# Port-order waits between VectorE and GpSimd, kept for the first half of the execution only, in a two-layer attention and MLP kernel

## The chip, the cores and the metric

The kernel runs on one core of a Trainium2 chip. A core has five engines with a queue of instructions each: TensorE (matrix products; the profile calls it PE, and its weight loads PEld), VectorE (DVE), ScalarE (ACT), GpSimd (POOL) and SyncE (SP), which here issues the DMAs. An engine works its own queue strictly in order; engines meet only through semaphores. SBUF is the on-chip memory that all of them use, PSUM the banks into which TensorE writes its products. The metric is the device time of one execution in microseconds (us), the median of several runs.

## The reference

Two kinds of layer alternate, attention (A) and MLP (B), each run twice with the same weights; the input `x` is 2048 tokens of 512 features in bf16.

```
def A(x, wqkv, wo):          # 32 heads of 16 features
    q, k, v = split(x @ wqkv)
    scores = (q . k) / 4
    mask: 0 <= query - key < 256         # a sliding window
    return softmax(masked scores) @ v, heads joined, @ wo
def B(x, w1, b1, w2, b2):    # 1792 hidden features
    return gelu(x @ w1 + b1) @ w2 + b2

x = x + A(layernorm(x)); x = x + B(layernorm(x))
x = x + A(layernorm(x)); x = x + B(layernorm(x))
```

## The kernel before, in words

The tokens are handled in 16 blocks of 256 (two tiles of 128), eight for each of the two layers. For a block, attention goes through *visits*. A visit computes 512 columns of scores for four heads at a time (TensorE, line 765), exponentiates them from PSUM into the SBUF tile `E` (ScalarE, two instructions of line 772), and multiplies the pieces of `E` at the window's edge with a 0/1 mask (line 793). That mask product reads two SBUF tiles, `E` and `mask01`. It runs on VectorE or, for the instructions listed in `_ALT`, on GpSimd. Then the probabilities meet the values (TensorE, line 817), VectorE transposes the result into `OD` (826), takes reciprocals of the sums (830), and `Nb = OD * Rc` is formed (834; VectorE or GpSimd). A transpose gives `OT` (840), and TensorE multiplies it with `Wo_sb` (line 664, as all the projections and the MLP). VectorE adds that to the residual `X` (866).

Layer norm is `bn_stats` and `bn_aggr` (616, 618, VectorE), the addition of epsilon (622; VectorE or GpSimd), a power of -0.5 on GpSimd (628), and the normalized tile `xn` on VectorE (638). `xn` is transposed by DMA (643), for the first and last tiles by TensorE (650) with a copy out of PSUM (605). The MLP's hidden tile `gT` gets bias and gelu on ScalarE (897), or bias on VectorE (889) and gelu on ScalarE (892). Its output is added on VectorE (909) to `Xb`, which GpSimd has prepared as `X` plus the bias `b2` (905).

The order of the work is written out. `_ORDER` is the order in which the 3080 steps are recorded, and with it each engine's queue; `_ALT` names the steps that go to the other engine; `_BANKS` the PSUM banks. The recording layer then puts a semaphore wait ahead of each instruction that reads or overwrites what another engine has made, unless an earlier wait already covers it.

`_TURNS` adds waits to this that no data needs. It is a flat list of pairs (a, z) of step numbers. For each pair, a is made to write a name that z reads, so that z waits for the end of a. In each pair one step is on VectorE and the other on GpSimd, and z is the later one in `_ORDER`. Nearly all the pairs are among mask products (793), `xn` (638), `Nb` (834), the epsilon step (622) and `Xb` (905). A step in several pairs stands in the list several times.

```
for a, z in zip(_TURNS[0::2], _TURNS[1::2]):
    nodes[a]["writes"] = nodes[a]["writes"] + ["turn%d" % z]
    nodes[z]["reads"] = nodes[z]["reads"] + ["turn%d" % z]
    nodes[z]["deps"].add(a)
```

Of the kernel before, what the change touches and what calls it, by code (L numbers as in the profile page):

```python
# [19 lines left out]
class _Sched:  # L20
# [339 lines left out]
]  # L360

_BANKS = [
# [618 lines left out]
```

## Time and profile before

| | |
|---|---|
| median of 3 runs | 440.76 us (440.29 to 441.36) |
| profiled execution | 440.62 us, of which the instructions span 438.9 us |
| busy: TensorE / ScalarE / VectorE / GpSimd | 424.2 / 385.6 / 341.0 / 201.1 us |
| TensorE clock granted | full throughout |
| mask products (793): VectorE / GpSimd | 122 with 51.0 us / 114 with 120.3 us |
| `xn` (638, VectorE), `Xb` (905, GpSimd) | 64 with 24.5 us / 32 with 36.8 us |

A row of the timeline gives the start (us from the span's start), the length, the engine, the line, the operation, the tiles written and read (out<-in) with their shapes, and how many instructions of that kind follow each other; in brackets, the engine's idle time before it and who ended it. A row of the groups by shape gives the count, total busy us and mean ns of one, and the idle time before these instructions with what ended it. A row of the waits gives who waited for whom, us in total, how many times, and the longest. "TENSOR_TENSOR E<-E,mask" is the mask product; its shape tells how many columns of `E` it covers.

### The profile page before, as it was taken

Reading aid. Unit: us, or ns where it says so; the run is one execution under the profiler, and the core shown is the slowest. Engines: PE = TensorE matmul, PEld = TensorE weight load, DVE = VectorE, ACT = ScalarE, POOL = GpSimd, SP = SyncE. Lnnn points to the kernel's source line nnn. Section 1 sums busy time; section 2 is a strip of 40 time slices with the busy share of each in tenths; the row PEclk is TensorE's granted clock in tenths of the full one; section 3 lists DMA queues with packets and bytes.
Section 4 is the critical chain, followed back from the end, with each engine's and each line's share of the span. In section 5 each row is a group of like instructions: output and inputs, shape, how many; then the busy total and the mean of one; then the engine's idle time right before and its main releaser. Section 6 shows DMA issues by size and latency. Waiting matters only on the chain.

```text
span 438.9 us, 16940 instructions
## 1 busy us (share of the span) xinstructions
PE 424.2 (97%) x7579; PEld 230.4 (52%) x7579; DVE 341.0 (78%) x647; ACT 385.6 (88%) x457; POOL 201.1 (46%) x224
## 2 busy tenths in 40 slices
PE   8989999999699989999999999999999999999997
PEld 4555756554344554454455555454564554544763
DVE  5999987799686889876899797877877686754852
ACT  3899999999999899999999988899888979899632
POOL 4366136464550275451854437743454515625222
PEclk9999999999999999999999999999999999999999
DMA  7772912002200102311030211201232022101011
GB/s 236 210 203 50 227 39 56 15 21 64 48 1 14 32 16 48 50 33 25 10 74 9 37 29 27 52 1 33 58 45 69 1 33 63 47 0 28 15 48 49
DMA packets 47972, 23.25 MB, mean 53 GB/s; under 512 B 33180, under 2 KB 47900, under 8 KB 47900
## 3 DMA queue, kind: packets, MB, share of 16 engines
q1 hardware_dynamic: 47900, 22.17, 21.8%
q8 instruction: 60, 0.98, 0.9%
q14 instruction: 12, 0.10, 0.1%
HBM read 8.00 MB, written 2.10 MB: 23 GB/s over the span
## 4 chain that ended last, share of the span: by engine, by line
PE 84%; ACT 8%; DVE 4%; DMA 3%; issue 1%; SPq 1%; POOL 0%; DVEq 0%
PE ps L664 65%; PE ps L765 10%; PE ps L817 8%; ACT E L772 7%; DMA W_sb<-in_B_w_dram 1%; DMA xnTB<-xn 1%; DVE stat L616 1%; DVE OD L826 1%; DVE KT L698 1%; DMA X<-in_A_x_dram 0%; PE ps L650 0%; DVE xn L638 0%; DVE X L909 0%; DVE X L866 0%; SPq L643 0%
## 5 line engine op out<-in xcount | busy, mean ns | idle before, releaser
L772 ACT ACTIVATE E<-ps 128x1024 bf16<-128x1024 f32 x300 | 283.2, 1040 | 25.6 <-PE ps L765 24.8
L793 POOL TENSOR_TENSOR E<-E,mask 128x512 bf16<-128x512 bf16 (+2 forms) x114 | 120.3, 1069 | 132.5 <-ACT E L772 52.7
L664 PE MATMUL ps<-W_sb,gT 128*128 128x512 bf16 x448 | 114.8, 380 | 0.1
L664 PE MATMUL ps<-xnTB,W_sb 128*128 128x512 bf16 (+1 forms) x560 | 109.3, 337 | 1.9 <-ACT E L772 1.5
L664 PEld LDWEIGHTS ps<-xnTB,W_sb 128*128 128x128 bf16 x560 | 51.9, 98 | 43.4 <-issue 4.6
L664 PE MATMUL ps<-xnTA,Wqkv_sb 128*128 128x256 bf16 x512 | 71.6, 273 | 1.2 <-ACT E L772 0.9
L765 PE MATMUL ps<-QT,KT 32*128 32x128 bf16 (+3 forms) x1920 | 60.4, 231 | 4.6 <-ACT E L772 2.6
L664 PEld LDWEIGHTS ps<-W_sb,gT 128*128 128x128 bf16 x448 | 39.4, 98 | 42.8 <-issue 4.0
L793 DVE TENSOR_TENSOR E<-E,mask 128x512 bf16<-128x512 bf16 (+2 forms) x122 | 51.0, 445 | 13.8 <-ACT E L772 11.6
L664 PEld LDWEIGHTS ps<-xnTA,Wqkv_sb 128*128 128x128 bf16 x512 | 46.6, 98 | 22.6 <-issue 3.3
L765 PEld LDWEIGHTS ps<-QT,KT 32*128 32x128 bf16 x1920 | 28.4, 92 | 52.6 <-ACT E L772 34.5
L826 DVE STREAM_TRANSPOSE OD<-ps 128x1024 f32<-128x1024 f32 x32 | 40.0, 1249 | 16.5 <-PE ps L817 14.6
L897 ACT ACTIVATE gT<-ps,b1T 128x512 bf16<-128x512 f32 (+1 forms) x80 | 43.0, 606 | 9.1 <-PE ps L664 9.0
L889 DVE TENSOR_SCALAR gT<-ps,b1T 128x512 bf16<-128x512 f32 (+1 forms) x60 | 36.7, 631 | 11.9 <-PE ps L664 11.4
L616 DVE BATCH_NORM_STATS2 stat<-X 128x6 f32<-128x512 bf16 x64 | 43.6, 687 | 3.0 <-DMA X<-in_A_x_dram 2.2
L905 POOL TENSOR_TENSOR Xb<-X,b2all 128x512 f32<-128x512 bf16 x32 | 36.8, 1154 | 13.1 <-DVE X L909 6.4
L817 PE MATMUL ps<-E,Va 64*17 64x256 bf16 (+3 forms) x1920 | 41.0, 230 | 1.8 <-DVE Va L605 0.5
L698 DVE TENSOR_TENSOR KT<-ps,parmask 128x1024 bf16<-128x1024 f32 x32 | 38.7, 1213 | 5.2 <-PE ps L664 5.0
L817 PE MATMUL ps<-E,Vs 64*17 64x192 bf16 (+3 forms) x1920 | 42.2, 230 | 0.0
L628 POOL TENSOR_TENSOR rstd<-rstd,mhalf 128x2 f32<-128x2 f32 (+1 forms) x33 | 24.2, 734 | 27.6 <-DVE rstd L622 23.3
L817 PEld LDWEIGHTS ps<-E,Va 64*17 64x17 bf16 x1920 | 29.2, 84 | 11.9 <-issue 8.3
L664 PE MATMUL ps<-Wo_sb,OT 128*128 128x512 bf16 x128 | 35.3, 380 | 0.1
(51 smaller groups left out, 350.1 us busy)
## 6 DMA issues: line engine op xcount, KB each, us to landing
Vs<-Va SPq DMA_DIRECT2D x64, 68.0 KB, 2.7
W_sb<-in_B_w_dram SPq DMA_DIRECT2D x4, 512.0 KB, 4.6
out_dram<-X SPq DMA_DIRECT2D x16, 128.0 KB, 1.8
X<-in_A_x_dram SPq DMA_DIRECT2D x3, 512.0 KB, 7.9
Wqkv_sb<-in_A_wqkv_dram SPq DMA_DIRECT2D x4, 256.0 KB, 5.5
W_sb<-in_B_w_dram SPq DMA_DIRECT2D x1, 768.0 KB, 5.2
W_sb<-in_B_w_dram SPq DMA_DIRECT2D x2, 384.0 KB, 5.0
Wqkv_sb<-in_A_wqkv_dram SPq DMA_DIRECT2D x1, 512.0 KB, 7.7
```

Of the source, the lines that this page charges most:

```text
L616: add("dve", lambda e, B, t=t, k6=k6: e.bn_stats(stat6[:, k6, :], X[:, t, :]), reads=["X%d" % t], writes=["st%d" % k6], key="bs%d" % (k + j))
L628: add("pool", lambda e, B, j=j, n=n: e.tensor_tensor(out=rstd[:, k + j : k + j + n], in0=rstd[:, k + j : k + j + n], in1=mhalf[:, 0:n], op ...
L664: r = e.matmul(ps[:, B[g][0], cols], lhsT, rhs, start=st, stop=sp)
L698: add("dve", lambda e, B, g=g, i=i: e.tensor_tensor(out=KT[:, kb, 2 * i : 2 * i + 2].rearrange("p c m a q -> p a (c m) q"), in0=ps[:, B[g] ...
L765: x = e.matmul(ps[:, bk[r], o : o + n], KT[rows, kb, c, m].rearrange("p a q -> p (a q)"), QT[rows, c, q : q + n], start=True, stop=True)
L772: add("act", lambda e, B, g_=g_, gi=gi: e.activation(E[:, 2 * gi : 2 * gi + 2, e0 : e0 + 512], ps[:, B[g_][0] : B[g_][0] + 2, :], AF.Exp, ...
L793: fn = lambda e, B: e.tensor_tensor(out=Ew, in0=Ew, in1=Mw, op=ALU.mult)
L817: x = e.matmul(ps[32 * r : 32 * r + VW, B[g][par], c % 2 * 2 * P + lo : c % 2 * 2 * P + hi], V[rows, (2 * b + m // 2) % VR, c * HC + 2 * r ...
L826: add("dve", lambda e, B: e.transpose(OD[:, s].rearrange("p a c q -> p (a c q)"), ps[:, B[g][0] : B[g][0] + 2, :]), reads=["ps:" + g], wri ...
L889: add("dve", lambda e, B, g=g, fc=fc: e.tensor_scalar(out=gT[:, fc, c0 : c0 + M], in0=ps[:, B[g][0], 0:M], scalar1=b1T[:, fc : fc + 1], sc ...
L897: add("act", lambda e, B, g=g, fc=fc: e.activation(gT[:, fc, c0 : c0 + M], ps[:, B[g][0], 0:M], AF.Gelu_apprx_tanh, bias=b1T[:, fc : fc + ...
L905: add("pool", lambda e, B, t=t, xs=xs: e.tensor_tensor(out=Xb[:, xs, :], in0=X[:, t, :], in1=b2all[:], op=ALU.add), reads=["X%d" % t, "b2a ...
```

## The change

The list `_TURNS` is cut after its 86th pair. The 86 pairs that stay lie in the first half of the execution: in the profiled execution of before, the last instruction that waits by one of them starts at 199.5 us, and the first that waited by one of the other 83 starts at 208.8 us. The loop above, `_ORDER`, `_ALT` and `_BANKS` are the same, so every engine has the same instructions in the same order.

```
-    1753, 1481, 1701, 1705, 1491, 1491, 1719, 1257, 1715, 1715, 1796, 1511, 1811, 1800, 1509, 1800, 1801, 1800, 1805,
-    1800, 1806, 1806, 1602, 1820, 1834, 1743, 1839, 1839, 2010, 2012, 2057, 2057, 1843, 1618, 2134, 1618, 2053, 1618,
...
-    2812, 2817, 2812, 2818, 2818, 2807, 2794, 2926, 2926, 2930, 2926, 2717, 2934, 2935, 2934, 2751, 2940, 2944, 2940,
-    2945, 2940, 2838, 2840, 2939, 2840, 2958, 2963, 2949, 2968, 2967, 2997, 2906, 2997, 2889,
+    1753,
 ]
```

By kind, the 83 pairs that go are: mask products on both engines 29, `xn` and a mask product 18, `Xb` and a VectorE step 18, `Nb` and a mask product 10, the epsilon step and a mask product 6, `xn` and `Nb` 2. Some of them put no wait into the program before, because another wait covered them: the waits that VectorE's queue holds on GpSimd go from 89 to 71, those that GpSimd's holds on VectorE from 98 to 71.

5 rows, old and new, of the table _TURNS are left out of this document.

## The prediction

> **What bounds the kernel now.** I read the page first (busy shares, then the chain that ended last), then the busy time of the half that the change touches, its waits, and last the timeline around single instructions.
>
> ```profile
> PE 424.2 (97%) x7579; PEld 230.4 (52%) x7579; DVE 341.0 (78%) x647; ACT 385.6 (88%) x457; POOL 201.1 (46%) x224
> ...
> PE 84%; ACT 8%; DVE 4%; DMA 3%; issue 1%; SPq 1%; POOL 0%; DVEq 0%
> ```
> ```profile
> 208.50:438.90 230.40, 227.06 (x3915) 120.11 (x3913) 167.14 (x312) 195.07 (x232) 106.67 (x105) 1.00 0.16 35
> ```
>
> The second row is the chain's share by engine; the third is the stretch from 208.5 us on: its length, then PE, PEld, DVE, ACT and POOL busy. TensorE sets the end: in that stretch it idles 230.40 - 227.06 = 3.3 us. Its queue has a fixed order, so a result that comes late for one matmul stops all that follow. VectorE (167 of 230 us) and GpSimd (107) have room on average; what counts is whether one of their results comes late for TensorE.
>
> **What the change removes.** Of the 169 pairs 83 go: in the profiled execution the first instruction freed starts at 208.8 us, the last at 424.0 (the list of pairs matched with the trace). Every engine keeps its order and no data wait goes, so unless the engines disturb each other, everything starts as early as before or earlier. What waits cost from 208.5 us on (who waited for whom: us in total, times, longest):
>
> ```profile
> POOL E L793 <- DVE E L793: 34.9, 11, 9.7
> ...
> POOL E L793 <- DVE xn L638: 7.0, 7, 2.5
> ...
> PEld ps L817 <- DVE E L793: 0.8, 2, 0.4
> ...
> PEld ps L817 <- POOL E L793: 0.2, 1, 0.2
> ```
>
> GpSimd's waits are long, but POOL is 0% of the chain: masks that start earlier are worth something only where TensorE waited for a mask. That is 0.8 + 0.2 = 1.0 us in this half, the most that can come back. Since nearly all the masks end before TensorE asks for them, I take 0.
>
> **What takes the waits' place.** They kept GpSimd's tile operations apart from those of VectorE that read two SBUF tiles (mask product, normalization `Nb`) and from the layer-norm `xn`. What happens when such instructions meet is seen at GpSimd's small rsqrt steps (L622, L628), which mostly have no such wait. First their spread (min/median/max ns), then two meetings:
>
> ```profile
> L628 POOL TENSOR_TENSOR rstd<-rstd,mhalf x33: 563/707/1138, 4.1 to 420.2; 128x2 f32<-128x2 f32 x31, 128x1 f32<-128x1 f32 x2
> ```
> ```profile
> L622 POOL TENSOR_SCALAR rstd<-statmv x16: 211/227/562, 3.8 to 354.2; 128x2 f32<-128x2 f32 x15, 128x1 f32<-128x1 f32 x1
> ```
> ```profile
> 319.47 0.42 DVE L793 TENSOR_TENSOR E<-E,mask 128x512 bf16<-128x512 bf16 x1
> ...
> 319.64 0.81 POOL L628 TENSOR_TENSOR rstd<-rstd,mhalf 128x2 f32<-128x2 f32 x1 [3.27 <-DVE rstd L622]
> ...
> 247.25 0.38 DVE L638 TENSOR_SCALAR xn<-X,statmv,rstd 128x512 bf16<-128x512 bf16 x1
> ...
> 247.42 0.29 POOL L622 TENSOR_SCALAR rstd<-statmv 128x2 f32<-128x2 f32 x1 [1.51 <-DVE statmv L618]
> ```
>
> The step that starts 0.17 us into a mask ends 0.56 us after that mask; the one 0.17 us into an `xn` ends 0.08 us after it. The steps are stretched to the end of VectorE's instruction and a rest, up to 1.138 us instead of 0.707. So one holds the other off entirely, at least when VectorE was first. The opposite case, a large GpSimd operation under way when VectorE's comes, does not occur in this trace: the waits prevented it. Its bounds: 0 (GpSimd holds nothing), or all that is left of GpSimd's operation, which is much longer:
>
> ```profile
> L793 POOL TENSOR_TENSOR E<-E,mask 128x512 bf16<-128x512 bf16 x60 | 68.9, 1154 | 62.0 <-ACT E L772 22.0 <-DVE Nb L834 16.3 <-DVE E L793 16.1
> L905 POOL TENSOR_TENSOR Xb<-X,b2all 128x512 f32<-128x512 bf16 x32 | 36.8, 1154 | 13.1 <-DVE X L909 6.4 <-DVE E L793 3.4 <-DVE xnTB L605 2.0
> ...
> L793 POOL TENSOR_TENSOR E<-E,mask 128x768 bf16<-128x768 bf16 x17 | 27.8, 1640 | 32.7 <-DVE E L793 13.7 <-DVE xn L638 9.1 <-ACT E L772 8.7
> ```
>
> I take nearly all of it, because the nearest rows are the same two engines with the roles exchanged and show a full hold. VectorE then stands for up to 1.64 us, with everything queued behind it, also operations that never met GpSimd. A held GpSimd instruction costs 0: it stands for the rest of a VectorE instruction (at most 0.7 us), where it now waits for several; what covers it is GpSimd's own idle time (230 - 107 us), and were that gone, each would cost those 0.7 us. Three groups of matmuls name a wait on GpSimd themselves that they had through VectorE before: the value was reached already, so 0.
>
> The Trainium skill's page "SBUF — State Buffer", section "Who interferes with whom", says the same of both directions: a VectorE instruction with two SBUF inputs contends with a GpSimd one that reads SBUF, and whoever issues first has the shared pair for the whole instruction. By that rule the sum is the forecast below; by the direction that the trace shows alone it would be that of the second rival. The trace agrees with it for VectorE first (0.81 us instead of 0.707), and has no row for GpSimd first.
>
> **Where it reaches TensorE.** Holds that TensorE does not notice are free. I went through the second half for places with little slack behind a VectorE instruction that a freed GpSimd operation can now stand before, and found five.
>
> A, 224 us:
> ```profile
> 223.35 1.14 POOL L628 TENSOR_TENSOR rstd<-rstd,mhalf 128x2 f32<-128x2 f32 x1 [1.85 <-DVE rstd L622]
> 225.08 2.75 POOL L793 TENSOR_TENSOR E<-E,mask 128x768 bf16<-128x768 bf16 x2 [0.59 <-DVE xn L638]
> ...
> 223.85 0.68 DVE L834 TENSOR_TENSOR Nb<-OD,Rc 128x512 bf16<-128x512 f32 x1
> 224.53 0.41 DVE L638 TENSOR_SCALAR xn<-X,statmv,rstd 128x512 bf16<-128x512 bf16 x1
> ...
> 225.45 0.71 DVE L840 STREAM_TRANSPOSE OT<-Nb 128x512 bf16<-128x512 bf16 x1
> ...
> 226.28 1.25 PE L664 MATMUL ps<-Wo_sb,OT 128*128 128x512 bf16 x5
> ```
> Freed, the 768-wide mask asks at 224.49, when the rsqrt ends, before `xn` at 224.53. `xn` waits up to 1.64 us; the transpose behind it ended at 226.16, 0.12 before its matmul. Cost 1.64 - 0.12 = 1.5 us (0 if `xn` wins).
>
> B, 268 us:
> ```profile
> 267.60 0.90 DVE L793 TENSOR_TENSOR E<-E,mask 128x768 bf16<-128x768 bf16 x2 [0.40 <-ACT E L772]
> 268.41 0.68 DVE L605 CAST QT<-ps 128x512 bf16<-128x512 f32 x1
> ...
> 268.64 2.75 POOL L793 TENSOR_TENSOR E<-E,mask 128x768 bf16<-128x768 bf16 x2 [2.90 <-DVE E L793]
> ...
> 269.43 1.04 PE L664 MATMUL ps<-xnTA,Wqkv_sb 128*128 128x256 bf16 x8
> ```
> GpSimd's mask comes in between VectorE's two: the second, and the QT cast behind it, wait some 1.5 us; the cast ended 269.09, 0.34 before the projection that needs its bank. Cost 1.2 us.
>
> C, 337 us:
> ```profile
> 336.44 0.69 DVE L834 TENSOR_TENSOR Nb<-OD,Rc 128x512 bf16<-128x512 f32 x1 [0.96 <-POOL E L793]
> 337.05 0.42 DVE L793 TENSOR_TENSOR E<-E,mask 128x512 bf16<-128x512 bf16 x1
> 337.38 0.70 DVE L840 STREAM_TRANSPOSE OT<-Nb 128x512 bf16<-128x512 bf16 x1
> ...
> 337.54 2.26 POOL L793 TENSOR_TENSOR E<-E,mask 128x768 bf16<-128x768 bf16 x2 [1.14 <-DVE E L793]
> ...
> 337.99 0.81 PE L664 MATMUL ps<-Wo_sb,OT 128*128 128x512 bf16 x3
> ```
> The 768-wide mask no longer waits for VectorE's mask, follows `Nb` at 337.13 and holds that mask, with the transpose behind it, for up to 1.64 us. The transpose ended at 338.08; if the last of the three output-projection matmuls is the first to need it (starts (0.81 - 0.38) / 2 = 0.21 us apart, with 0.38 for one as at D, so 338.42), the slack is 0.34. Cost 1.3 us.
>
> D, 408 us:
> ```profile
> 407.26 1.39 DVE L793 TENSOR_TENSOR E<-E,mask 128x768 bf16<-128x768 bf16 x4
> ...
> 408.79 1.15 POOL L793 TENSOR_TENSOR E<-E,mask 128x512 bf16<-128x512 bf16 x1 [4.70 <-DVE E L793]
> ...
> 411.45 0.63 ACT L892 ACTIVATE gT<-gT 128x512 bf16<-128x512 bf16 x1 [1.25 <-DVE gT L889]
> ...
> 412.41 0.38 PE L664 MATMUL ps<-W_sb,gT 128*128 128x512 bf16 x1
> ```
> GpSimd's mask falls among VectorE's four; the last moves by about 1.15, so do the bias adds, and the gelu that waits for them. It ended at 412.08, 0.33 before the matmul: 0.8 us.
>
> E, 421 us, on the chain itself:
> ```profile
> 420.89 0.74 DVE L638 TENSOR_SCALAR xn<-X,statmv,rstd 128x512 bf16<-128x512 bf16 x2 [0.80 <-POOL rstd L628]
> ...
> 422.87 2.27 POOL L905 TENSOR_TENSOR Xb<-X,b2all 128x512 f32<-128x512 bf16 x2 [2.02 <-DVE xnTB L605]
> ```
> The Xb add now follows the rsqrt that releases `xn` directly, and stands before the first or the second `xn`; TensorE transposes both next. Cost 1.13 us (2.3 if both adds get in).
>
> Sum: 1.5 + 1.2 + 1.3 + 0.8 + 1.1 = 5.9 us. The profiled execution took 440.62 us (span 438.9 and 1.7 around it), 0.14 below the median 440.76: 440.62 + 5.9 = 446.5 us. DMAs, ScalarE's work and bytes are unchanged and cost 0: what is late is the same work, hidden as before.
>
> **The rivals.**
> - A weaker hold: GpSimd holds VectorE for part only, or VectorE wins half the races. 0.2 to 0.6 of 5.9: 1.2 to 3.5 us, 441.8 to 444.1. Against it: L628's maximum is a complete hold.
> - No hold by GpSimd: VectorE goes on beside it. Then the gain's bound remains, 0 to 1.0 us and the noise: 440.0 to 441.4. For it: only VectorE's hold is seen.
> - Faster: GpSimd's masks at A to D end up to 1 us earlier, and this ends TensorE's waits for masks, 1.0 us: 439.6. It decides only if the holds cost TensorE under 0.1 us. Against it: E, where there is nothing to gain and 1.1 to lose.
> - The change does nothing, because the pairs are implied by other waits: partly so, since in the programs VectorE's waits on GpSimd fall only from 89 to 71 and GpSimd's on VectorE from 98 to 71, which leaves 45 waits that do go; where none of these mattered, the time would be the second rival's.
>
> **How the numbers follow.** About 0.2% (0.9 us) is what a measurement can tell from no change. Forecast (near-full hold, 444.1 to 449.3; the upper end takes 1.5, 1.5, 1.6, 1.15 and 2.3 = 8.1, and 0.6 for smaller places): 0.56. Weaker hold 0.18, no hold or no effect 0.16, faster 0.08, above 449.3 0.02. Slower is 0.56 + 0.18 + 0.02 = 0.76. The range leaves out the fastest and slowest ends: 440.3 to 449.3.
>
> **What would show it.** Right: from 208.5 us on, VectorE instructions of the three kinds end with, or just after, a GpSimd operation, or take longer than now; the matmuls at A to E start later by the sums given, in steps; TensorE's idle time in the stretch grows from 3.3 to about 9 us; the first 208 us stay. Wrong: GpSimd's masks overlap VectorE's with unchanged durations, or `xn` at A and E goes first each time.

## The result, and the profile after

| | before | after |
|---|---|---|
| median | 441.01 us (440.29 to 442.90, 6 runs) | 447.56 us (446.89 to 449.50, 6 runs) |
| ratio | | 1.0152, 95% interval 1.0122 to 1.0183 |
| profiled execution (span) | 440.62 (438.9) us | 446.97 (445.2) us |

The change costs 6.5 us by the medians and 446.97 - 440.62 = 6.35 us between the profiled executions; forecast was 5.9. The page of the changed kernel, its lines 8 lower (630 is `xn`, 785 the mask product, 897 `Xb`):

```profile
PE 425.4 (96%) x7579; PEld 230.0 (52%) x7579; DVE 356.0 (80%) x647; ACT 385.9 (87%) x457; POOL 204.0 (46%) x224
...
PE 76%; DVE 11%; ACT 10%; DMA 1%; issue 1%; POOL 1%; SPq 0%; DVEq 0%
...
L785 DVE TENSOR_TENSOR E<-E,mask 128x512 bf16<-128x512 bf16 (+2 forms) x122 | 57.9, 501 | 12.3 <-ACT E L764 12.0
...
L630 DVE TENSOR_SCALAR xn<-X,statmv,rstd 128x512 bf16<-128x512 bf16 x64 | 32.5, 527 | 4.3 <-POOL rstd L620 3.8
```

VectorE is busy for 15.0 us more with the same 647 instructions: 6.9 of them in the mask products (57.9 against 51.0 before) and 8.0 in `xn` (32.5 against 24.5). VectorE's share of the chain went from 4 to 11%. The two halves (length, then PE, PEld, DVE, ACT, POOL busy):

```profile
0.00:208.10 208.10, 196.86 (x3666) 110.41 (x3667) 173.93 (x336) 190.56 (x227) 94.40 (x119) 1.00 0.31 73
208.10:445.20 237.10, 228.51 (x3915) 119.58 (x3913) 182.10 (x312) 195.35 (x232) 109.55 (x105) 1.00 0.16 34
```

All of the extra is in the second: VectorE 182.1 against 167.1 us, TensorE's idle time 237.10 - 228.51 = 8.6 against 3.3. TensorE's busy time is 1.2 us longer too (425.4 against 424.2, the same matmuls); no run here shows why. The spread of the two kinds of VectorE instructions (min/median/max ns) shows how: the median stayed (407 and 420 before), the longest `xn` went from 415 to 1728, the longest mask product from 560 to 1859.

```profile
L630 DVE TENSOR_SCALAR xn<-X,statmv,rstd x64: 316/407/1728, 5.4 to 427.0; 128x512 bf16<-128x512 bf16 x64
```
```profile
L785 DVE TENSOR_TENSOR E<-E,mask x122: 229/422/1859, 20.3 to 412.6; 128x512 bf16<-128x512 bf16 x56, 128x768 bf16<-128x768 bf16 x47, 128x256 bf16<-128x256 bf16 x19
```

The timeline of the changed kernel at the prediction's places, A to E in turn:

```profile
224.62 1.72 DVE L630 TENSOR_SCALAR xn<-X,statmv,rstd 128x512 bf16<-128x512 bf16 x1
...
224.55 2.79 POOL L785 TENSOR_TENSOR E<-E,mask 128x768 bf16<-128x768 bf16 x2
...
227.61 1.25 PE L656 MATMUL ps<-Wo_sb,OT 128*128 128x512 bf16 x5 [1.46 <-DVE OT L832]
...
268.74 2.33 DVE L785 TENSOR_TENSOR E<-E,mask 128x768 bf16<-128x768 bf16 x2 [0.33 <-ACT E L764]
...
268.78 5.04 POOL L785 TENSOR_TENSOR E<-E,mask 128x768 bf16<-128x768 bf16 x4 [2.07 <-ACT E L764]
...
271.73 1.05 PE L656 MATMUL ps<-xnTA,Wqkv_sb 128*128 128x256 bf16 x8 [1.00 <-DVE QT L597]
...
339.19 1.86 DVE L785 TENSOR_TENSOR E<-E,mask 128x512 bf16<-128x512 bf16 x1
...
335.96 5.60 POOL L785 TENSOR_TENSOR E<-E,mask 128x768 bf16<-128x768 bf16 x4 [7.79 <-ACT E L764]
...
341.72 0.61 PE L656 MATMUL ps<-Wo_sb,OT 128*128 128x512 bf16 x2 [1.04 <-DVE OT L832]
...
411.52 2.35 DVE L785 TENSOR_TENSOR E<-E,mask 128x768 bf16<-128x768 bf16 x4
...
412.28 1.44 POOL L785 TENSOR_TENSOR E<-E,mask 128x512 bf16<-128x512 bf16 x1 [3.88 <-ACT E L764]
...
416.67 0.63 ACT L884 ACTIVATE gT<-gT 128x512 bf16<-128x512 bf16 x1 [2.31 <-DVE gT L881]
...
425.84 2.39 DVE L630 TENSOR_SCALAR xn<-X,statmv,rstd 128x512 bf16<-128x512 bf16 x2 [0.80 <-POOL rstd L620]
...
425.77 2.31 POOL L897 TENSOR_TENSOR Xb<-X,b2all 128x512 f32<-128x512 bf16 x2
...
427.13 0.40 PE L642 MATMUL ps<-ident,xn 128*128 128x128 bf16 x4 [0.50 <-DVE xn L630]
...
428.29 0.40 PE L642 MATMUL ps<-ident,xn 128*128 128x128 bf16 x4 [0.55 <-DVE xn L630]
```

At A the mask starts 0.07 us ahead of `xn`, and `xn` takes 1.72 us instead of 0.41; the output projection, which came at once before, now finds TensorE idle for 1.46 us behind VectorE's transpose. At B VectorE's two masks take 2.33 instead of 0.90 us, at C one takes 1.86 instead of 0.42, at D four take 2.35 instead of 1.39 and the gelu behind their bias adds waits 2.31 instead of 1.25, at E the two `xn` take 2.39 instead of 0.74.

TensorE's work has the same order in both kernels, so each group of matmuls can be matched and its end compared. The difference hardly changes but for a few steps (us of the execution before; change of the difference):

| place | 0 to 208 | A 227 | 231 | B 270 | C 339 | 379 to 385 | D 402 to 413 | E 422 | sum |
|---|---|---|---|---|---|---|---|---|---|
| step, us | -0.3 | +1.6 | -0.2 | +1.2 | +1.2 | +0.8 | +0.7 | +1.4 | +6.4 |
| forecast | 0 | 1.5 | | 1.2 | 1.3 | | 0.8 | 1.1 | 5.9 |

The first half, where nothing was changed, has a step of -0.3 here and of +0.3 in the first kernel of the next section: that much is spread between executions.

### The profile page after: what moved, and what is told of

It reads as the page before. It is cut to its first block, busy times and chain, and to the rows that moved or that the text cites. A ratio compares the mean times of both kernels' runs of the same rounds, so it can differ in the third digit from the quotient of the medians.

```text
span 445.2 us, 16919 instructions
## 1 busy us (share of the span) xinstructions
PE 425.4 (96%) x7579; PEld 230.0 (52%) x7579; DVE 356.0 (80%) x647; ACT 385.9 (87%) x457; POOL 204.0 (46%) x224
## 4 chain that ended last, share of the span: by engine, by line
PE 76%; DVE 11%; ACT 10%; DMA 1%; issue 1%; POOL 1%; SPq 0%; DVEq 0%
PE ps L656 58%; ACT E L764 9%; PE ps L757 9%; PE ps L809 8%; DVE E L785 2%; DVE gT L881 2%; DVE xn L630 1%; DVE OD L818 1%; DVE stat L608 1%; DMA xnTB<-xn 1%; DVE Nb L826 1%; DVE X L858 1%; DVE OT L832 1%; DVE X L901 1%; DMA X<-in_A_x_dram 0%
## 5 line engine op out<-in xcount | busy, mean ns | idle before, releaser
L785 POOL TENSOR_TENSOR E<-E,mask 128x512 bf16<-128x512 bf16 (+2 forms) x114 | 123.3, 1094 | 125.1 <-ACT E L764 98.2
L785 DVE TENSOR_TENSOR E<-E,mask 128x512 bf16<-128x512 bf16 (+2 forms) x122 | 57.9, 501 | 12.3 <-ACT E L764 12.0
L630 DVE TENSOR_SCALAR xn<-X,statmv,rstd 128x512 bf16<-128x512 bf16 x64 | 32.5, 527 | 4.3 <-POOL rstd L620 3.8
```

The lines of the kernel that those rows point to most:

```text
L630: add("dve", lambda e, B: e.tensor_scalar(out=xn[:, s, :], in0=X[:, t, :], scalar1=statmv[:, k, 0:1], scalar2=rstd[:, k : k + 1], op0=ALU. ...
L785: fn = lambda e, B: e.tensor_tensor(out=Ew, in0=Ew, in1=Mw, op=ALU.mult)
```

## The experiments

The theory is that VectorE's three kinds of instructions and GpSimd's operations exclude each other on a port of SBUF that both engines use, that whoever comes second stands until the first is done, and that the loss arises where a freed GpSimd operation comes first and TensorE has little slack behind VectorE. The rivals: every meeting costs alike, whoever was to wait; the loss is spread over many small holds; GpSimd's other start times are themselves the trouble. In the edits `n` is the number of the pair in the list and z the step that waits; each is made in the loop over `_TURNS` of the kernel before, unless told otherwise.

**Which side's waits carry it.** First the pairs of the second half in which GpSimd waits:

```
+for n, (a, z) in enumerate(zip(_TURNS[0::2], _TURNS[1::2])):
+    if n >= 86 and nodes[z]["eng"] == "pool":
+        continue
```

> Of the second half's 83 pairs only the 37 in which GpSimd waits are dropped; the 46 in which VectorE waits stay. Port theory: the loss comes from GpSimd's operations that now get in ahead of a VectorE instruction and hold it; all the pairs whose order turned round in the changed kernel's trace are of this kind, so this alone costs what the whole change costs: 5.5 to 8 us over the kernel before, 446.5 to 449. Rival, that every meeting costs alike, whoever was to wait: 37/83 of 6.5 us, 2.9 us, 444.

Measured: 448.57 us against 440.80, ratio 1.0168 (1.0146 to 1.0190), 7.4 us by the ratio: the whole loss, within the intervals. Then the other part:

```
+    if n >= 86 and nodes[z]["eng"] == "dve":
```

> The opposite part: only the 46 pairs in which VectorE waits are dropped. Port theory: where VectorE would have waited for the end of a GpSimd operation, the port holds it until about the same moment, so nothing changes: within 0.5 us of the kernel before, 440.5 to 441.5. Rival, that every meeting costs alike: 46/83 of 6.5 us, 3.6 us, 444.6.

Measured: 440.62 against 440.80, ratio 1.0003 (0.9988 to 1.0018). From 208.1 us on (columns as above):

```profile
208.10:438.40 230.30, 226.98 (x3915) 119.85 (x3913) 169.56 (x312) 195.16 (x232) 106.95 (x105) 1.00 0.16 35
```

VectorE is busy 2.4 us longer than before in this half (169.56 against 167.14), which fits its standing now in instructions where it used to wait for a semaphore; TensorE's idle time is the same 3.3 us. So the rival of equal costs falls. Nothing here is lost when VectorE is held where it was to wait anyway; all is lost where GpSimd gets in ahead.

The same with both halves, keeping only the 80 pairs in which GpSimd waits (`if nodes[z]["eng"] == "dve"`):

> Of all 169 pairs, in both halves, only the 80 in which GpSimd waits stay; the 89 in which VectorE waits are dropped. Port theory: VectorE's waits are the port's own, so the kernel runs as before, 440.3 to 441.3, with half the pairs. Rival, that the second half's result does not carry over to the first, where VectorE's waits are the more: 442 or more.

Measured: 441.60 against 441.06, ratio 1.0007 (0.9993 to 1.0020): no change that can be told, though the median lies 0.3 us above the range expected. 89 of the 169 pairs are worth at most 0.2% (0.9 us), and nothing that these runs can tell.

**Whether a few places carry it.** The changed kernel with seven pairs put back:

```
+    if n >= 86 and n not in (91, 111, 141, 154, 166, 167, 168):
```

> The changed kernel with 7 of its 83 dropped pairs put back: one each at 224, 268, 337, 378 and 409 us and two at 421 us of the execution before, where TensorE's shift jumps. Port theory with the places of the prediction: the steps there (1.6 + 1.2 + 1.2 + 0.8 + 0.3 + 1.4 = 6.5 us) go, the other 76 pairs are worth next to nothing: 441 to 443. Rival, that the loss is spread over many small holds: 7/83 of it comes back, 447.

Measured: 442.76 against 440.80, ratio 1.0045 (1.0033 to 1.0058), so 4.6 of 6.5 us come back; within the range given. The steps at A to E are gone, but there are two others, 0.87 us at 231 and 0.55 at 385, where other dropped pairs meet now. The timeline of this kernel (`xn` is line 640, `Xb` 907, masks 795):

```profile
227.83 1.31 DVE L640 TENSOR_SCALAR xn<-X,statmv,rstd 128x512 bf16<-128x512 bf16 x1
...
227.84 1.16 POOL L907 TENSOR_TENSOR Xb<-X,b2all 128x512 f32<-128x512 bf16 x1
...
382.66 0.89 DVE L795 TENSOR_TENSOR E<-E,mask 128x512 bf16<-128x512 bf16 x1
...
382.11 1.16 POOL L795 TENSOR_TENSOR E<-E,mask 128x512 bf16<-128x512 bf16 x1 [0.85 <-ACT E L774]
```

Put the two pairs that order GpSimd there back as well (96 and 156), nine in all:

> The kernel with seven pairs put back had two new steps of TensorE's, 0.87 us at 231 us and 0.55 us at 385 us. Here the two pairs that order GpSimd there are put back as well, nine of 83. Port theory: both steps go, and the rest of the second half's pairs are worth 0 to 0.5 us together: 440.8 to 441.6. Rival, that each place put right shifts the loss to another: 442 to 443 as with seven.

Measured: 441.35 against 441.06, ratio 1.0007 (0.9990 to 1.0023). Nine of 83 pairs do what the 83 did, as far as these runs can tell (at most 0.23%, 1.0 us, is left), and the loss did not move elsewhere. Many holds of VectorE remain in that kernel; three rows of it, the stretch from 208.1 us on and one place:

```profile
208.10:439.00 230.90, 227.53 (x3935) 120.11 (x3918) 174.76 (x313) 195.44 (x232) 108.41 (x105) 1.00 0.16 35
```
```profile
320.66 2.88 DVE L640 TENSOR_SCALAR xn<-X,statmv,rstd 128x512 bf16<-128x512 bf16 x2 [0.26 <-POOL rstd L630]
...
320.59 4.44 POOL L795 TENSOR_TENSOR E<-E,mask 128x512 bf16<-128x512 bf16 x3
```

VectorE is busy 174.8 us where it was 167.1, so 7.6 us of holds stay, two `xn` that take 2.88 us among them; TensorE idles 3.4 us as before. These holds cost nothing, since TensorE does not wait for what stands behind them.

**One place at a time.** The kernel before without the one pair at A (`if n == 91`):

> The kernel before without a single one of its 169 pairs, that at 224 us, where GpSimd's 768-wide mask product waits for VectorE's xn (place A). Port theory: the mask stands before xn, which then takes about 1.7 us instead of 0.41, and TensorE's output projection comes 1.3 to 1.6 us later for good: 442.1 to 442.6. Rival, that a single hold is taken up by later slack: within 0.5 us of before.

Measured: 441.77 against 441.06, ratio 1.0013 (0.9997 to 1.0028), 0.6 us. The hold is there, in the size expected:

```profile
224.47 1.72 DVE L640 TENSOR_SCALAR xn<-X,statmv,rstd 128x512 bf16<-128x512 bf16 x1
...
227.46 1.25 PE L666 MATMUL ps<-Wo_sb,OT 128*128 128x512 bf16 x5 [1.18 <-DVE OT L842]
```

TensorE's step is 1.2 us, of which 0.3 are made up later in this trace; the span is 439.8 us against 438.9. So the expectation missed in size: it took a step for a loss for good. By the interval the loss is between 0 and 1.2 us; the two traces say 0.9. Without the two pairs at E (`if n in (167, 168)`):

> The kernel before without the two pairs at 421 us (place E), where GpSimd's two additions for Xb wait. Port theory: each xn takes about 1.23 us instead of 0.41, TensorE's two transposes move by 0.7 us each, 442.0 to 442.4. Rival, slack behind it: within 0.5 us of before.

Measured: 442.15 against 441.06, ratio 1.0030 (1.0015 to 1.0045), 1.3 us, with steps of 0.6 and 0.7 at TensorE's two transposes:

```profile
423.70 0.40 PE L652 MATMUL ps<-ident,xn 128*128 128x128 bf16 x4 [0.50 <-DVE xn L640]
...
424.86 0.40 PE L652 MATMUL ps<-ident,xn 128*128 128x128 bf16 x4 [0.55 <-DVE xn L640]
```

Neither step is made up later in this trace: behind E there is no slack left.

**All pairs, and the other half.** None of the 169 (`if n >= 0`), and the first 86 dropped with the last 83 kept (`if n < 86`):

> None of the 169 pairs. Port theory: the first half loses too, where GpSimd's freed operations stand before VectorE with little slack behind; from replaying the order of the trace by hand 3 to 5 us more than the changed kernel, 450 to 453. Rival, that the first half has slack because attention alone runs there: within 1 us of the changed kernel.

> The other half: the first 86 pairs are dropped, the last 83 stay. Port theory, costs of places adding up: none of the pairs cost 451.4 - 440.8 = 10.6 us over before, the changed kernel 6.5 of them, so this one 4.1: 444.4 to 445.4. Rival, that halves do not add, since what is late in the first half gives slack to the second: 2 us or less.

Measured: 451.43 against 440.80, ratio 1.0235 (1.0209 to 1.0261), and 445.50 against 441.94, ratio 1.0087 (1.0055 to 1.0119). The first half costs 0.87% (the median lies 0.1 us above the range expected), the second 1.52%, together 2.39%; all at once 2.35%. Within these intervals the halves add.

**What a hold is.** The changed kernel with each of the two `Xb` additions at E cut in two:

```
-e.tensor_tensor(out=Xb[:, xs, :], in0=X[:, t, :], in1=b2all[:], op=ALU.add)
+def prep(e, B, t=t, xs=xs, tau=tau):
+    for lo, hi in ((0, 256), (256, 512)) if tau in (28, 29) else ((0, 512),):
+        r = e.tensor_tensor(out=Xb[:, xs, lo:hi], in0=X[:, t, lo:hi], in1=b2all[:, lo:hi], op=ALU.add)
+    return r
```

> The changed kernel, but at 421 us (place E) each of GpSimd's two additions for Xb is cut into two of 256 columns. Port theory: a hold lasts as long as the single GpSimd instruction under way; a 256-column operation takes about 0.67 us instead of 1.15, so each xn takes about 0.75 us instead of 1.23, and TensorE's two steps shrink from 1.4 to 0.3 to 0.7 us: about 0.9 us below the changed kernel. Rival, that VectorE stands until GpSimd's queue has nothing more to do: each xn as long as before or longer, no gain.

Measured: 446.78 against 441.94, ratio 1.0111 (1.0087 to 1.0134).

```profile
426.73 1.42 DVE L640 TENSOR_SCALAR xn<-X,statmv,rstd 128x512 bf16<-128x512 bf16 x2 [0.80 <-POOL rstd L630]
...
426.65 2.64 POOL L909 TENSOR_TENSOR Xb<-X,b2all 128x256 f32<-128x256 bf16 x4
```

The two `xn` take 1.42 us instead of 2.39, although GpSimd goes on adding for 1.1 us after they are done, and TensorE's steps at E shrink from 1.4 to 0.4 us. So a hold lasts as long as the one operation under way, and then VectorE gets its turn. The ratio lies below that of the changed kernel, with intervals that overlap; the trace is what shows it.

The same two operations as memsets, which read nothing:

```
+    e.memset(idle[:, tau - 28, :], 0.0)      # a spare tile, 304 columns
+    return e.memset(Xb[:, xs, :], 0.0)
```

> The changed kernel, but at 421 us (place E) GpSimd's two additions for Xb are replaced by memsets (a spare tile, then the Xb buffer), which read nothing from SBUF and are free as early; X and b2 are left out of the MLP's output for two tiles, so the output is not the reference's there. Port theory in the form that it is GpSimd's reading that holds VectorE: xn takes 0.41 us each beside the memsets, and TensorE's two steps there (0.68 and 0.72 us) go: 1.4 us below the changed kernel. Port theory in the form that any GpSimd operation holds an xn: each xn ends about 0.15 us after a memset, and part of the steps stays. Rival, that GpSimd's starting there early is itself the trouble: the steps stay in full with xn at 0.41 us.

Measured: 447.62 against 441.94, ratio 1.0129 (1.0104 to 1.0154).

```profile
427.89 1.94 DVE L641 TENSOR_SCALAR xn<-X,statmv,rstd 128x512 bf16<-128x512 bf16 x2 [0.80 <-POOL rstd L631]
...
427.80 0.35 POOL L911 MEMSET idle<- 128x304 f32 x1
...
428.85 0.52 POOL L912 MEMSET Xb<- 128x512 f32 x1
```

The first `xn` takes 1.62 of the 1.94 us and ends 0.15 us after the last of the four memsets, the second takes 0.41; TensorE keeps a step of 1.1 us. So it is not GpSimd's reading that holds an `xn`: the first form of the expectation falls, and the second holds only in part: the hold passes from one memset to the next without a turn for VectorE. The rival falls too, as `xn` did not keep 0.41 us.

For a mask product the opposite came out. At D, GpSimd's one mask product is replaced by three memsets (the spare tile twice, then the same piece of `E`):

> The changed kernel, but at 412 us (place D) GpSimd's one 512-column mask product is replaced by three memsets (two on a spare tile, one on the same piece of E), which read nothing; that piece of E is zeroed instead of masked, so the output is not the reference's. At place E four memsets in a row held an xn for 1.62 us. If any operation of GpSimd holds any of VectorE's three kinds: the last of VectorE's four masks ends about 0.15 us or a little more after the last memset, 1 us or more instead of 0.28, and TensorE's steps there (0.37 and 0.28 us) stay. If a mask product, which needs only to read two tiles, is held by GpSimd's reading alone and xn by its writing too: all four masks keep 0.28 to 0.42 us beside the memsets, and the steps go, 0.6 us below the changed kernel.

Measured: 447.99 against 440.71, ratio 1.0153 (1.0115 to 1.0192); the medians cannot tell 0.6 us here.

```profile
413.84 1.39 DVE L796 TENSOR_TENSOR E<-E,mask 128x768 bf16<-128x768 bf16 x4
...
414.58 0.64 POOL L800 MEMSET idle<- 128x304 f32 x2 [3.89 <-ACT E L775]
415.16 0.52 POOL L801 MEMSET E<- 128x512 bf16 x1
```

VectorE's four masks take 1.39 us, as before the change, with memsets running beside the last two; in the changed kernel they took 2.35. TensorE's steps at D are gone from the trace. So here, in one place each, a mask product is held by a GpSimd operation that reads, and not by one that only writes.

The Trainium skill's page "SBUF — State Buffer", section "Who interferes with whom", has these two cases as rules: two SBUF inputs contend only with a GpSimd instruction that reads, and a VectorE instruction in a mode that uses both ports contends with any. The rows agree (1.39 us unheld, 1.62 us held), if `xn` runs in such a mode, which no run here shows by itself.

## Why the prediction was right

- *What bounds it, and no gain from the waits that go.* Right. In the second half no wait of GpSimd for VectorE's masks or `xn` is left, but its masks that start earlier brought TensorE nothing: small steps of -0.2 at 231 and 402 us aside, no step of the second half is a gain.
- *The hold works both ways.* This was the step without a row of its own, argued from VectorE holding GpSimd. It holds: `xn` takes 1.72 us beside a 1.64 us mask, and it ends 0.15 us after GpSimd's operation; in the kernel with seven pairs back so does an `xn` that begins, by the record, within 0.01 us of GpSimd's operation (227.83 + 1.31 against 227.84 + 1.16). "Nearly all" of what is left of GpSimd's operation was the right end of the bounds. The rule that the prediction cites from the Trainium skill ("SBUF — State Buffer", "Who interferes with whom") did not carry the whole sum: it is for VectorE instructions with two SBUF inputs, and `xn` has one tile and two values per partition as inputs. So the 1.5 + 1.1 us at A and E did not follow from it; the runs show them.
- *The places.* The steps at A, B, C and E lie within 0.3 us of the forecast, and GpSimd won each race, also the close ones (0.07 us at A and E). B and C came nearly as worked out (a mask held for 1.86 - 0.42 = 1.44 us at both, where the sums had 1.5 and 1.64). At A and E the working was off and the fit is luck. At A the hold added 1.72 - 0.41 = 1.31 us, not 1.64; less the slack of 0.12 this is the 1.2 us that the kernel without that one pair shows. The step of 1.6 is larger because VectorE came to `xn` 0.09 us later than before (224.62 against 224.53) and TensorE was 0.2 us early. At E both additions got in, for which the prediction had 2.3 us; but each stood before one `xn` only and held it for 0.82 us (1.23 instead of 0.41), so the two steps of 0.7 make 1.4. The forecast 1.1 was for one addition that holds for its whole length. D came with 0.7 instead of 0.8, of which 0.5 stand at the two groups of matmuls behind VectorE's masks (410 and 412 us). The sum fits partly by luck too: 0.8 us at 379 to 385 were not foreseen (a VectorE mask product that took 1.05 us at 380 us of the changed kernel, and bias adds behind it), and 0.5 us of opposite sign, in the first half and at 231, made up for most of that.
- *C in detail.* `Nb` was held as well, by the mask ahead of it, for 1.56 us; but it would have waited for that mask before, so this cost nothing, and the mask product behind it carried the step.
- *The rivals.* A weaker hold would have given 441.8 to 444.1, no hold 440.0 to 441.4; the lengths of the held instructions exclude both. The faster one falls, since the masks that start earlier gave TensorE no gain above those 0.2 us. The fourth was half right. Dropping the 46 pairs of the second half in which VectorE waits changed nothing that can be told, and VectorE's waits on GpSimd fell by only 18 in the changed kernel, so many of these pairs were implied by other waits; for the others the hold does what the wait did. The pairs in which GpSimd waits carry the loss.
- *What would show it.* TensorE's idle time was to grow to about 9 us; it grew to 8.6. The first half stayed, within 0.3 us.

## What to carry to other kernels

Where two engines hold each other off, as VectorE and GpSimd do here, a semaphore on top changes only who goes first. Here it was worth having where the long operation of the slower engine would otherwise get in just ahead of a short one that the bounding engine waits for, and nowhere else that these runs can tell: nine pairs did the work of 83. So look for places where the slack behind the short instruction is less than the length of the long one. Where a hold cannot be avoided, cutting the long operation into pieces may help: at E it made the two `xn` 1.42 us instead of 2.39, while GpSimd's additions took 2.64 instead of 2.31.

## What was not expected of the hardware

- A held `xn` ends 0.15 us after GpSimd's operation, though it takes 0.41 alone; held masks end 0.15, 0.28 and 0.42 us after it for 256, 512 and 768 columns (0.28, 0.42 and 0.55 alone). So VectorE goes on some 0.13 us, `xn` 0.26 us, before the recorded end of GpSimd's operation. The estimate with the whole rest was too high for that. The prediction's rows already had it with VectorE first: the two small GpSimd steps ended 0.56 and 0.08 us after VectorE's instruction, where their medians are 0.707 and 0.227, so 0.15 us less in each case.
- In these rows GpSimd's reading operations and VectorE take turns (four additions of 256 columns, two `xn`), while four memsets in a row let no `xn` in between. Why is not shown.
- In the profiled executions of four versions (memsets at E, memsets at D, first half's pairs dropped, the pairs at E dropped) TensorE's mean granted clock from 118 to 124 us is 0.72 instead of 1.00. That is a mean: in the version with memsets at E the clock is 0.50 from 119.5 to 122.5 us and 1.00 from 123 us on. TensorE falls some 1.5 us behind there. Executions of the kernel before have the same mean clock over the whole span (0.995 to 0.996), so it does not come from the change; it adds to the spread of the runs, and steps under 1 us are read from traces here. The two rows, from the version with memsets at E, give the clock as the third figure from the right:

```profile
118.00:124.00 6.00, 5.15 (x45) 2.03 (x47) 2.89 (x7) 3.90 (x5) 3.28 (x4) 0.72 0.11 26
119.50:122.50 3.00, 3.00 (x31) 1.11 (x30) 0.79 (x2) 1.45 (x3) 1.78 (x3) 0.50 0.03 8
```

No version measured here is faster than the kernel before by more than the runs can tell.
